# Routed attention and a gelu feed-forward on one Trainium2 core: rounding the weights one operation at a time instead of in blocks

## The chip, the core and the metric

The kernel runs on one core of one Trainium2 chip. A core has a matrix engine (TensorE, in the profile PE, with its weight loads shown as PEld), a vector engine (VectorE, DVE), a scalar engine for activations and copies (ScalarE, ACT), a general engine (GpSimd, POOL) and an engine that issues most transfers (SyncE, SP). They run side by side, each through its own list of instructions in order, and wait for one another through semaphores. On-chip data lies in SBUF; matrix products land in PSUM[...]. The metric is the device time of the whole program in microseconds (us). The kernel before takes 1042.07 us, the median of three runs (1040.81 to 1043.41).

## The reference

What is computed is this:

```python
# q, k, v: (4, 8, 768, 64); centroids: (8, 16, 64)
q_assign = argmax(einsum('bhsd,hcd->bhsc', q_n, c_n))      # nearest centroid
k_assign = argmax(einsum('bhsd,hcd->bhsc', k_n, c_n))
mask = q_assign[:, :, :, None] == k_assign[:, :, None, :]
scores = where(mask, q @ k.T / sqrt(64), -1e9)
attn = softmax(scores) @ v
x = attn.transpose(0, 2, 1, 3).reshape(3072, 512)
h = x @ w_in                                               # 512 x 2048
out = (h / (1 + exp(-1.702 * h))) @ w_out                  # 2048 x 512
```

So there are 4 batches of 8 heads. A query attends only to the keys that share its cluster, and the result goes through a feed-forward block with a quick gelu.

## The kernel before, in words

**Layout.** Heads are handled in pairs; a pair with half of its 768 queries is a group (`g`), and a group has six units (`u`), one for each block of 128 keys. The main loop (L608 to L654) goes through *turns*: each turn `t` takes two units. There are 96 turns, 24 to a batch, 3 to a group. In a turn TensorE does, in this order: the two units' scores (L397), for the first batch the products that bring in the mask (`part`, L411), the products with v of the turn before (`values`, L454), and then pieces of other work: the sums of a group (`normalise`, L466), transposes and centroid products that prepare coming pairs (`prep`, L275 to L345), and pieces of the feed-forward block (`ffn`).

**Beside TensorE.** ScalarE takes exps of the scores (L422). GpSimd adds the exps of a group up (L443, `sum`, 128x768, one addition in a group's first turn and two in its others). From the second batch on VectorE applies the mask (L433). After a group's last unit, TensorE sums over partitions, VectorE takes a reciprocal (L469) and multiplies (L471).

**Feed-forward of the first half batch.** `ffn_half` runs from turn 14, at 1.6 pieces a turn: 16 pieces `first(f)` (L516 to L526) of four matrix products (L520), each followed by a gelu: tanh on ScalarE (L490), then one VectorE operation (L491) that reads the product's PSUM bank; and then 12 pieces `second3` (L528), the products with w_out (L500). The bank pool `ps_m` (tile name `m`) has three banks for all of this: products of the feed-forward, transposes, the group sums. A product can start when an earlier user's last reader has released its bank.

**Rounding of the weights.** The weights come in as 64-bit numbers, in 32 chunks of 128x512 (16 of w_in, then 16 of w_out). `round_next` (L165) rounds one chunk with four VectorE operations: L175 (shift and mask the high half), L178 (put in sign and exponent, two SBUF inputs), L180 (mask out the power of two), L183 (the low half times that power, two SBUF inputs), and one addition (L185) that makes the weight. At its start it asks for the chunk after next (`load_w(i + 2)`, into one of three `raw` buffers), and at its end it puts two checks on ScalarE (`check_w`, L196 and L199). For the last chunk the check writes over the raw data itself. In the eight chunks of turns 0 to 13 the addition is on VectorE. From turn 14 it is on GpSimd, and each turn rounds two chunks: one at the top of the turn, right after the exps (L622), one at the very end (L653), until all 32 are done, in turn 25. Nothing reorders the instructions afterwards (`manual_schedule`): on each engine they stand as the Python code issues them.

The stream of VectorE in turns 14 to 25 is thus: four rounding operations, the mask (from turn 24), the reciprocal (turns 16, 19, 22, 25), an assignment (`prep_assign`, L306 to L329, in turns 21 and 24), one or two gelus, four rounding operations. GpSimd's is: the addition of the top chunk, the exp sums of the turn, the addition of the end chunk.

**After the loop.** The other batches' feed-forward (`first7` and `second7`, L746 and L803) runs when the attention is through.

Of the kernel before, what the change touches and what calls it, by code (L numbers as in the profile page):

```python
# [38 lines left out]
def fast(  # L39
# [26 lines left out]
    nc = tc.nc  # L66
# [40 lines left out]
    def bank():  # L107
        return ps_m.tile([P, 512], FP32, name="m")

    def short():  # L110
        return tmp.tile([P, HALF], FP32, name="short")
# [14 lines left out]
    def load_v(p):  # L126
        b, hp = divmod(p, HP)
        t = pairs.tile([P, 2, NJ, D], FP32, name="inv")
        nc.sync.dma_start(
            out=t.rearrange("p a j d -> p a (j d)"),  # L130
            in_=v[b, 2 * hp:2 * hp + 2].rearrange(
                "a (p j) d -> p a (j d)", j=NJ))
        v_in[p] = t
# [15 lines left out]
    NW = len(w_chunks)  # L149
    w_raw, w_pow = {}, {}  # L150

    def load_w(i):
        if i < NW:
            t = wp.tile([P, WN, 2], I32, name="raw")
            nc.sync.dma_start(out=t.rearrange("p n t -> p (n t)"),
                              in_=w_chunks[i][1])
            w_raw[i] = t
# [4 lines left out]
    POWER = -2 ** 23  # L162
    w_done = [0]

    def round_next(in_psum=False, engine=nc.gpsimd):  # L165

        i = w_done[0]
        if i == NW:
            return
        load_w(i + 2)  # L170
        raw, w = w_raw.pop(i), w_chunks[i][0]
        e = wp.tile([P, WN], I32, name="e", bufs=2)
        a = bank() if in_psum else w
        hi, lo, a_i = raw[:, :, 1], raw.bitcast(U32)[:, :, 0], a.bitcast(I32)
        nc.vector.tensor_scalar(out=a_i, in0=hi, scalar1=3, scalar2=0x3FFFFFF8,  # L175
                                op0=ALU.logical_shift_left,
                                op1=ALU.bitwise_and)
        nc.vector.scalar_tensor_tensor(out=a_i, in0=hi, scalar=ODD, in1=a_i,  # L178
                                       op0=ALU.bitwise_and, op1=ALU.bitwise_or)
        nc.vector.tensor_scalar(out=e, in0=a_i, scalar1=POWER, scalar2=None,  # L180
                                op0=ALU.bitwise_and)
        e = e.bitcast(FP32)
        nc.vector.scalar_tensor_tensor(out=e, in0=lo, scalar=2.0 ** -52, in1=e,  # L183
                                       op0=ALU.mult, op1=ALU.mult)
        engine.tensor_tensor(out=w, in0=a, in1=e, op=ALU.add)  # L185

        check_w(i, raw, w_chunks[NW - 1][0] if i < NW - 1 else raw.bitcast(
            FP32)[:, :, 1])
        w_done[0] += 1

    def check_w(i, raw, z):

        nc.scalar.activation(out=z, in_=raw.bitcast(FP32)[:, :, 1],  # L196
                             func=AF.Square,
                             accum_out=row_sums[:, 2, i:i + 1])
        nc.scalar.activation(out=z, in_=z, func=AF.Exp, scale=-2.0 ** 12,  # L199
                             bias=fifteen[:, 0:1],  # L200
                             accum_out=row_sums[:, 3, i:i + 1])

    def round_to(n):
        while w_done[0] < n:
            round_next()

    load_qk(1, 0)
    load_v(0)
# [252 lines left out]
    def normalise(g):  # L461

        sm = sum_of.pop(g)
        ps = bank()
        for a in range(2):
            nc.tensor.matmul(out=ps[a * D:(a + 1) * D, 0:HALF], lhsT=twos,  # L466
                             rhs=sm[:, a, :], start=True, stop=True)
        rec = recs[g] = short()
        nc.vector.reciprocal(out=rec, in_=ps[:, 0:HALF])  # L469
        x = xT_of[g] = O_of.pop(g)  # L470
        nc.vector.tensor_tensor(out=x, in0=x, in1=rec, op=ALU.mult)  # L471
        if g % HP == HP - 1 and g < 2 * HP:
            (half_ffn, ffn)[g // HP].extend((ffn_half, ffn_tiles)[g // HP]())
# [14 lines left out]
    def gelu(g, t, h):  # L488

        nc.scalar.activation(out=t, in_=h, func=AF.Tanh, scale=1.702)  # L490
        nc.vector.scalar_tensor_tensor(out=g, in0=t, scalar=1.0, in1=h,  # L491
                                       op0=ALU.add, op1=ALU.mult)
# [5 lines left out]
    def second(bh, n, f, g, ps):  # L498

        nc.tensor.matmul(out=ps[:, 0:DM], lhsT=g, rhs=w_out[:, f, :],  # L500
                         start=(f == 0), stop=(f == NF - 1))
        if f == NF - 1:
            b, h = divmod(bh, 2)
            y = yp.tile([P, DM], FP32, name="y")
            nc.scalar.copy(y, ps[:, 0:DM])
            nc.sync.dma_start(out=out_rows(b, h, n), in_=y)

    half_ffn, ffn = deque(), deque()

    def ffn_half():  # L510


        xT = [xT_of.pop(c) for c in range(NCH)]
        gs, ys = {}, {}

        def first(f):  # L516
            round_to((f * P // WN + 1) * NCH)
            ps = bank()
            for c in range(NCH):
                nc.tensor.matmul(out=ps[:, 0:HALF],  # L520
                                 lhsT=w_in[:, c, f * P:(f + 1) * P],
                                 rhs=xT[c], start=(c == 0),
                                 stop=(c == NCH - 1))
            g = gs[f] = (xp.tile([P, HALF], FP32, name="x") if f % 4 else
                         gp.tile([P, 4 * P], FP32, name="g")[:, 0:HALF])
            gelu(g, g, ps[:, 0:HALF])  # L526

        def second3(n, part):  # L528
            round_to(NW // 2 + 4 * (part + 1))
            if part == 0:  # L530
                ys[n] = bank()
            for f in range(4 * part, 4 * part + 4):
                second(0, n, f, (gs.pop(f) if n == NH - 1 else gs[f])[
                    :, n * P:(n + 1) * P], ys[n])

        return ([lambda f=f: first(f) for f in range(NF)]
                + [lambda n=n, q=q: second3(n, q)
                   for n in range(NH) for q in range(NF // 4)])
# [33 lines left out]
    NT = NU // 2  # L572
    TG = NJ // 2
    TB = 2 * HP * TG

    prep_at = {}
    for p in range(1, NPAIR):
        b, hp = divmod(p, HP)
        for i in range(2 if p == 1 else 0, len(PREP)):
            if p == 1:  # L580
                t = (i - 2) // 2
            elif b == 0:
                t = (hp - 2) * TG + 1 + i // 2
            else:
                t = b * TB + TG * hp - (7, 7, 6, 6, 4, 3, 2)[i]
# [5 lines left out]
    def prep(p, i):  # L591
        if i == 0 and p:
            load_v(p)
        PREP[i](p)
        if i in (1, 3) and loads:
            load_qk(*loads.popleft())

    rate = 1.6


    pace = {t: 1 for t in (0, 2, 5, 8, 9, 11, 12, 13)}
    pace.update((t, 2) for t in range(TB // 2 + 2, NT))
    owed = 0.0
    for p, i in [(0, i) for i in range(6)] + [(1, i) for i in range(2)]:
        prep(p, i)
# [2 lines left out]
    for t in range(NT + 2):  # L608
        us = range(2 * t, 2 * t + 2) if t < NT else ()
        for u in us:  # L610
            scores(u)
        if t == 0:
            prep(0, 6)
        for u in us:
            part(u)
        for u in us:
            exps(u)
        second_half = t >= TB // 2
        how = ((False, nc.gpsimd) if t >= TB // 2 + 2 else
               (t > 2, nc.vector))  # L620
        late = t <= 2 or t == TB // 2 + 1
        if pace.get(t) and not late:  # L622
            round_next(*how)
        if recs:
            check(*recs)
        for u in us:
            mask(u)
        work = sorted(prep_at.get(t, ()), key=lambda w: PREP[w[1]] != prep_near)
        while work and PREP[work[0][1]] == prep_near:
            prep(*work.pop(0))  # L630
        if 1 <= t <= NT:
            for u in range(2 * t - 2, 2 * t):
                values(u)

        kept = NF // 2 if t < NT - 3 else NF // 4
        todo = half_ffn or (ffn if len(ffn) > kept else ())
        if not todo:
            owed = 0.0
        elif half_ffn:
            owed += rate  # L640
        else:
            owed += 0.65 if t < NT - 3 else 1.0
        g = (t - 2) // TG if t >= 2 and (t - 2) % TG == TG - 1 else None
        if g is not None and second_half:
            normalise(g)
        for p, i in work:
            prep(p, i)
        if g is not None and not second_half:
            normalise(g)
        while owed >= 1 and todo:  # L650
            todo.popleft()()
            owed -= 1
        if pace.get(t) == 2 or pace.get(t) and late:  # L653
            round_next(*how)  # L654
    check(*recs)
    qcode.clear()
    att.close()
# [648 lines left out]
```

## Time and profile before

| Engine | busy us | share of 1040.6 us |
| --- | --- | --- |
| TensorE (PE) | 993.8 | 96% |
| VectorE (DVE) | 681.7 | 66% |
| GpSimd (POOL) | 418.6 | 40% |
| ScalarE (ACT) | 372.8 | 36% |

| Group | count | mean ns |
| --- | --- | --- |
| L175 on w_out chunks | 16 | 574 |
| L178 on w_out chunks | 16 | 1354 |
| L180 on w_out chunks | 16 | 426 |
| L183, all chunks | 32 | 876 |
| L491 gelu, 128x384 into x | 12 | 550 |
| L469 reciprocal | 32 | 2552 |
| L443 sums (sum<-sum,A) | 128 | 1834 |

Busy times are of the whole span; a TensorE that is busy in the profile is not at its peak all the time, since the ends of its pipelined products are modelled. The turns that concern the change lie between about 86 and 208 us on VectorE; TensorE works on a turn some us before VectorE does. The prediction shows lines of that stretch. In the timelines, columns are: start in us, duration in us, engine, line of the kernel, operation, tile written and tiles read, shapes, how many; in brackets, how long the engine stood idle ahead of it and who ended the wait.

### The profile page before, as it was taken

What the parts mean: (1) busy time and instruction counts of PE and PEld (TensorE: products, weight loads), DVE (VectorE), ACT (ScalarE), POOL (GpSimd) and SP (SyncE); (2) the same over time, 40 slices, a digit from 0 to 9 for tenths busy, and PEclk for the clock granted to TensorE, in tenths of its full rate; (3) what the DMA queues carried; (4) which work ended last, traced back from release to release, by engine and by line L of the source; (5) the groups of instructions that cost most, each with busy time, mean ns of one, the idle gap of its engine ahead of it and who ended that gap; (6) DMA issues with size and microseconds to landing.
All of it is one profiled execution on the core that took longest, in us unless ns stands there. A gap on an engine that the chain in (4) does not pass through costs nothing.

```text
span 1040.6 us, 12560 instructions
## 1 busy us (share of the span) xinstructions
PE 993.8 (96%) x4574; PEld 583.8 (56%) x4574; DVE 681.7 (66%) x1055; ACT 372.8 (36%) x761; POOL 418.6 (40%) x304
## 2 busy tenths in 40 slices
PE   7999888989999999999999999999999999999997
PEld 4434434434554435544454355688755788656886
DVE  4699987844777687677777667744377634576431
ACT  4676564432445544554545222200022100222000
POOL 2574654523566556565666757500022100120000
PEclk9999898999999999999999999999999999999999
DMA  8423544310003310220000000000000000000000
GB/s 222 129 61 101 155 135 136 107 41 18 19 17 76 92 41 2 57 71 27 26 1 1 11 1 0 1 21 21 21 0 1 1 21 21 21 0 1 21 21 23
DMA packets 66118, 45.25 MB, mean 43 GB/s; under 512 B 52096, under 2 KB 60032, under 8 KB 66048
## 3 DMA queue, kind: packets, MB, share of 16 engines
q1 hardware_dynamic: 65904, 44.33, 14.9%
q8 instruction: 38, 0.62, 0.3%
q14 instruction: 32, 0.26, 0.1%
q10 hardware_dynamic: 144, 0.03, 0.0%
HBM read 38.04 MB, written 6.31 MB: 43 GB/s over the span
## 4 chain that ended last, share of the span: by engine, by line
PE 83%; DVE 13%; ACT 2%; issue 1%; DMA 0%; POOL 0%; DVEq 0%; ACTq 0%
PE b L803 21%; PE b L746 21%; PE s L397 11%; PE o L454 10%; PE m L500 7%; PE m L549 4%; PE m L520 3%; PE m L275 2%; DVE short L469 2%; DVE e L183 2%; PE m L466 2%; DVE w_out L178 1%; DVE e L180 1%; DVE A L433 1%; DVE w_in L178 1%
## 5 line engine op out<-in xcount | busy, mean ns | idle before, releaser
L443 POOL TENSOR_TENSOR sum<-sum,A 128x768 f32<-128x768 f32 x128 | 234.7, 1834 | 133.8 <-DVE A L433 115.3
L433 DVE SCALAR_TENSOR_TENSOR A<-qb,code,s 128x384 f32<-128x384 uint8 x288 | 157.4, 608 | 89.4 <-ACT s L422 52.6
L397 PE MATMUL s<-T,T 64*128 64x384 f32 x768 | 154.1, 514 | 2.9 <-DVE A L433 0.6
L454 PE MATMUL o<-A,inv 128*64 128x384 f32 x768 | 145.1, 499 | 1.0 <-ACT x L459 1.0
L422 ACT ACTIVATE s<-s 128x768 f32<-128x768 f32 x144 | 109.0, 793 | 99.5 <-PE s L397 87.1
L737 DVE TENSOR_TENSOR G<-b,G 128x384 f32<-128x384 f32 x168 | 93.4, 556 | 48.3 <-PE b L746 41.4
L684 POOL TENSOR_TENSOR W<-w_in 128x256 f32<-128x256 f32 x24 | 17.7, 738 | 261.0 <-PE b L746 259.3
L490 ACT ACTIVATE th<-G 128x384 f32<-128x384 f32 x96 | 50.2, 523 | 163.4 <-DVE G L737 103.0
L397 PEld LDWEIGHTS s<-T,T 64*128 64x128 f32 x768 | 65.7, 187 | 75.6 <-issue 34.0
L737 DVE TENSOR_TENSOR y<-b,y 128x256 f32<-128x256 f32 x54 | 22.1, 423 | 130.0 <-PE b L803 93.5
L746 PE MATMUL b<-x,w_in 128*128 128x384 f32 x288 | 101.3, 487 | 0.0
L454 PEld LDWEIGHTS o<-A,inv 128*64 128x64 f32 x768 | 46.6, 136 | 85.1 <-issue 81.4
L469 DVE RECIPROCAL short<-m 128x384 f32<-128x384 f32 x32 | 81.7, 2552 | 7.2 <-PE m L466 7.1
L443 POOL TENSOR_TENSOR sum<-A 128x768 f32<-128x768 f32 x32 | 58.8, 1836 | 63.7 <-DVE A L433 32.5
L491 DVE SCALAR_TENSOR_TENSOR G<-th,G 128x384 f32<-128x384 f32 x96 | 68.6, 714 | 16.8 <-ACT th L490 14.2
L746 PEld LDWEIGHTS b<-x,w_in 128*128 128x128 f32 x288 | 54.9, 191 | 37.8 <-issue 0.5
L746 PE MATMUL b<-x,W 128*128 128x384 f32 x192 | 70.7, 492 | 0.0
L803 PE MATMUL b<-Z,G 128*128 128x256 f32 x288 | 65.1, 380 | 0.0
L803 PE MATMUL b<-w_out,G 128*128 128x256 f32 x288 | 63.6, 380 | 0.0
L500 PE MATMUL m<-w_out,g 128*128 128x512 f32 x120 | 60.0, 619 | 2.2 <-ACT T L280 2.2
L520 PE MATMUL m<-x,w_in 128*128 128x384 f32 x128 | 49.3, 542 | 10.3 <-DVE short L309 5.2
L803 PEld LDWEIGHTS b<-w_out,G 128*128 128x128 f32 x288 | 54.7, 190 | 7.9
(126 smaller groups left out, 1343.2 us busy)
## 6 DMA issues: line engine op xcount, KB each, us to landing
raw<-in_moe_w_in_dram SPq DMA_DIRECT2D x16, 512.0 KB, 4.8
raw<-in_moe_w_out_dram SPq DMA_DIRECT2D x16, 512.0 KB, 3.6
in<-in_q_dram SPq DMA_DIRECT2D x32, 192.0 KB, 4.2
in<-in_k_dram SPq DMA_DIRECT2D x32, 192.0 KB, 3.2
inv<-in_v_dram SPq DMA_DIRECT2D x16, 384.0 KB, 4.2
out_dram<-y SPq DMA_DIRECT2D x15, 256.0 KB, 2.5
qb<-line SPq DMA_DIRECT2D x12, 192.0 KB, 3.3
out_dram<-y SPq DMA_DIRECT2D x18, 128.0 KB, 1.8
```

What stands on the lines that cost most here:

```text
L397: nc.tensor.matmul(out=ps[:, a, 0:HALF], lhsT=T[p, 1][rows, kt * P:(kt + 1) * P], rhs=T[p, 0][rows, h * HALF:(h + 1) * HALF], start=True, ...
L422: nc.scalar.activation(out=A_of[u] if p < HP else s, in_=s, func=AF.Exp, scale=SCALE)
L433: nc.vector.scalar_tensor_tensor(out=A_of[u][:, a, :], in0=qcode[p][:, a, h * HALF:(h + 1) * HALF], scalar=code[p][:, kt % NH, 1, kt // NH ...
L443: nc.gpsimd.tensor_tensor(out=sum_of[g], in0=A_of[u - 1] if kt == 1 else sum_of[g], in1=A, op=ALU.add)
L454: nc.tensor.matmul(out=o_of[g][a * D:(a + 1) * D, 0:HALF], lhsT=v_in[p][:, a, kt, :], rhs=A[:, a, :], start=(kt == 0), stop=(kt == NJ - 1))
L469: nc.vector.reciprocal(out=rec, in_=ps[:, 0:HALF])
L491: nc.vector.scalar_tensor_tensor(out=g, in0=t, scalar=1.0, in1=h, op0=ALU.add, op1=ALU.mult)
L500: nc.tensor.matmul(out=ps[:, 0:DM], lhsT=g, rhs=w_out[:, f, :], start=(f == 0), stop=(f == NF - 1))
L520: nc.tensor.matmul(out=ps[:, 0:HALF], lhsT=w_in[:, c, f * P:(f + 1) * P], rhs=xT[c], start=(c == 0), stop=(c == NCH - 1))
L737: nc.vector.tensor_tensor(out=o, in0=p, in1=a, op=ALU.add)
L746: nc.tensor.matmul(out=ps[:, 0:HALF], lhsT=a[:, c], rhs=x(c), start=(c == 0), stop=(c == 1))
L803: nc.tensor.matmul(out=ps[:, 0:DN], lhsT=a(f // 4)[:, f % 4], rhs=z(f), start=(f == 0), stop=(f == FB - 1))
```

## The change

Rounding becomes a generator that hands over one VectorE operation at a time; `step` takes the next one, and the fourth brings the addition and the checks with it. From turn 14 each turn gets a budget of eight steps, as many as two chunks need. `advance(n)` takes up to n of them, and is called at many places of the turn: two steps at the top, one after `normalise`, one after each preparation, three between a feed-forward product and its gelu, two after each feed-forward piece. Before turn 14 a chunk is still rounded in one go. The purpose is to place the rounding where VectorE would wait for TensorE, and to let gelus, reciprocals and preparations not stand behind whole blocks.

```diff
-    def round_next(in_psum=False, engine=nc.gpsimd):
+    def rounding(in_psum, engine):
...
         nc.vector.tensor_scalar(out=a_i, in0=hi, scalar1=3, scalar2=0x3FFFFFF8,
...
+        yield
         nc.vector.scalar_tensor_tensor(out=a_i, in0=hi, scalar=ODD, in1=a_i,
...
+        yield
         nc.vector.tensor_scalar(out=e, in0=a_i, scalar1=POWER, scalar2=None,
...
+        yield
...
         w_done[0] += 1
+        yield
...
+    steps = [0]
+    def advance(n):
+        while n and steps[0] > 0:
+            step()
+            steps[0] -= 1
+            n -= 1
...
+            advance(3)
             gelu(g, g, ps[:, 0:HALF])
...
-    pace.update((t, 2) for t in range(TB // 2 + 2, NT))
...
-        how = ((False, nc.gpsimd) if t >= TB // 2 + 2 else
-               (t > 2, nc.vector))
+        if t > TB // 2 + 1:
+            steps[0] += 8
         late = t <= 2 or t == TB // 2 + 1
         if pace.get(t) and not late:
-            round_next(*how)
+            round_next(True, nc.vector)
+        advance(2)
...
         if g is not None and second_half:
             normalise(g)
+        advance(1)
         for p, i in work:
             prep(p, i)
+            advance(1)
...
         while owed >= 1 and todo:
             todo.popleft()()
             owed -= 1
-        if pace.get(t) == 2 or pace.get(t) and late:
-            round_next(*how)
+            advance(2)
+        if pace.get(t) and late:
+            round_next(t > 2, nc.vector)
```

With it the streams of turns 14 to 25 become, R being one rounding operation, N the reciprocal and its multiplication, A the assignment, M the masks, g a gelu:

```
turn   before            after
14     4R g 4R           6R g 2R
15     4R gg 4R          6R g 2R g
16     4R N g 4R         2R N 4R g 2R
17     4R gg 4R          8R gg
18     4R gg 4R          8R gg
19     4R N g 4R         2R N 4R g 2R
20     4R gg 4R          8R gg
21     4R A g 4R         3R A 5R g
22     4R N gg 4R        2R N 5R g R g
23     4R gg 4R          8R gg
24     4R M A 4R         2R M R A 5R
25     4R M N 4R         2R M N 6R
```

On GpSimd, the exp sums of a turn now stand ahead of both of its weight additions instead of between them.

More of the change, by code (lines that the diff above doesn't have):

```diff
@@ L163, in fast @@
     w_done = [0]
-    def round_next(in_psum=False, engine=nc.gpsimd):
+    def rounding(in_psum, engine):
         i = w_done[0]
-        if i == NW:
-            return
         load_w(i + 2)
@@ L189, in round_next, with step @@
         w_done[0] += 1
+        yield
+    now = []
+    def step(*how):
+        if not now and w_done[0] < NW:
+            now.append(rounding(*(how or (False, nc.gpsimd))))
+        if now:
+            n = w_done[0]
+            next(now[0])
+            if w_done[0] > n:
+                now.clear()
+    def round_next(*how):
+        n = w_done[0]
+        while w_done[0] == n < NW:
+            step(*how)
     def check_w(i, raw, z):
@@ L204, in round_to @@
         while w_done[0] < n:
-            round_next()
+            step()
     load_qk(1, 0)
@@ L508, in fast @@
     half_ffn, ffn = deque(), deque()
+    steps = [0]
+    def advance(n):
+        while n and steps[0] > 0:
+            step()
+            steps[0] -= 1
+            n -= 1
     def ffn_half():
```

## The prediction

> **What bounds the kernel now.** I read the page's slices first, then summed the engines over the turns that the diff touches, then the chain of work, then the VectorE and GpSimd timelines of those turns side by side. From about 215 us on the chain is TensorE almost without a break (TensorE 83% of the span, VectorE 13%), so only what moves the start of that tail moves the end. The slices show where VectorE is fullest and the TensorE clock dips: the third to the eighth of the 40 slices, 52 to 208 us.
>
> ```profile
> PE   7999888989999999999999999999999999999997
> DVE  4699987844777687677777667744377634576431
> PEclk9999898999999999999999999999999999999999
> ```
>
> VectorE issues the first rounding operation of turn 14 at 86.36 us and the last chunk's second one (L178) at 207.90, ended 208.60. Summed over nearly that stretch (columns: window, its length, then busy us and instructions of TensorE, its weight loads, VectorE, ScalarE, GpSimd; clock, DMA share, GB/s):
>
> ```profile
> 86.36:207.45 121.09, 104.06 (x438) 49.44 (x436) 106.92 (x135) 64.92 (x153) 68.01 (x43) 0.93 0.44 132
> ```
>
> VectorE is 88% busy. But the busy time is not all work. The two timelines (start us, us, engine, line) show one block of turn 14:
>
> ```profile
> 88.63 0.55 DVE L491 SCALAR_TENSOR_TENSOR g<-g,m 128x384 f32<-128x384 f32 x1
> 89.09 1.26 DVE L175 TENSOR_SCALAR w_in<-raw 128x512 int32<-128x512 int32 x1
> 90.38 2.19 DVE L178 SCALAR_TENSOR_TENSOR w_in<-raw,w_in 128x512 int32<-128x512 int32 x1
> 92.60 1.92 DVE L180 TENSOR_SCALAR e<-w_in 128x512 int32<-128x512 int32 x1
> 94.56 0.69 DVE L183 SCALAR_TENSOR_TENSOR e<-raw,e 128x512 f32<-128x512 uint32 x1
> 95.17 0.42 DVE L175 TENSOR_SCALAR w_in<-raw 128x512 int32<-128x512 int32 x1
> 95.63 1.65 DVE L178 SCALAR_TENSOR_TENSOR w_in<-raw,w_in 128x512 int32<-128x512 int32 x1
> 97.38 0.43 DVE L180 TENSOR_SCALAR e<-w_in 128x512 int32<-128x512 int32 x1
> ```
>
> ```profile
> 88.79 1.28 POOL L185 TENSOR_TENSOR w_in<-w_in,e 128x512 f32<-128x512 f32 x1 [8.04 <-DVE e L183]
> 90.03 4.21 POOL L443 TENSOR_TENSOR sum<-sum,A 128x768 f32<-128x768 f32 x2
> 95.33 1.40 POOL L185 TENSOR_TENSOR w_in<-w_in,e 128x512 f32<-128x512 f32 x1 [1.09 <-DVE e L183]
> ```
>
> L175 takes 0.42 alone and 1.26 beside GpSimd's add; L178 0.69 and 2.19; L180 0.43 and 1.92: each held operation ends 0.3 to 0.7 us after a GpSimd operation does. The two engines take turns. The gelu L491 reads PSUM and keeps its 0.55. Going through 86.36 to 208.60 operation by operation, time above each operation's shortest is 29.7 us; idle time of VectorE is 9.9 us, in five gaps, each the tanh of a product that TensorE began late, as here (the second line is TensorE's own gap before it):
>
> ```profile
> 163.75 0.56 DVE L491 SCALAR_TENSOR_TENSOR x<-x,m 128x384 f32<-128x384 f32 x1 [3.35 <-ACT x L490]
> ```
>
> ```profile
> 158.36 4.83 PE L520 MATMUL m<-x,w_in 128*128 128x384 f32 x8 [5.16 <-DVE short L309]
> ```
>
> So of 122.2 us, 82.6 are work that no order removes, and 39.6 are held or waiting. The stretch is handed to the tail by ScalarE: the last chunk's check overwrites its own raw data, so it waits for L178 at 208.60, and the exps and copies behind it hold TensorE until 213.35:
>
> ```profile
> 208.63 0.69 ACT L196 ACTIVATE raw<-raw 128x512 f32<-128x512 f32 x1 [10.34 <-DVE w_out L178]
> ```
>
> TensorE itself stands still 21.4 us between 76 and 225 us, so it could run earlier if VectorE did.
>
> **What the Trainium skill says.** "SBUF — State Buffer", section "Who interferes with whom": a VectorE instruction with two SBUF inputs, or a tensor_scalar in a two-port mode, shares an exclusive lock with GpSimd; whoever comes first keeps it for its whole instruction, and an instruction with at most one SBUF input outside those modes isn't held. The trace agrees: 0.43 against 1.92 us for L180, 0.55 always for L491. "Perfetto Trace Analysis", section "GPSIMD Engine Instruction": GpSimd spans are to be timed by the spacing of starts. I therefore take 1.24 us for an add (88.79 to 90.03) and about 1.85 for a sum.
>
> **The change part by part.** The same 96 operations run in turns 14 to 25, eight a turn in both, and TensorE's order and its three `m` banks are the same through turn 23. No instruction is added. Three things move.
>
> (a) Reciprocals (turns 16, 19, 22, 25) and the assignments of turns 21 and 24 stand behind 2 or 3 rounding operations instead of 8. The product of turn 21 waited for the assignment's L309 until 158.22. In the new order, carrying my times below forward, L309 ends near 157.6, TensorE starts there, and five rounding operations fill VectorE until the tanh: the 3.35 us gap shrinks to about 0.35. Of the other gaps (0.64, 1.82, 2.08, 2.03) I keep one of 1.4 in turn 22, before the reciprocal, and fill the rest, since eight operations (or six, in the middle of a split pair) now stand ahead of every first gelu. Idle: 9.9 to 1.75, a gain of 8.1.
>
> (b) First gelus of turns 17 and 20 get ten operations between them and the gelu before (8 before), since two are left over from the reciprocal turn. They come up to 5 us later, and gelus free the banks. But the next turn's bank is wanted only after two products, scores and values, 5.4+3.5 us, so TensorE loses little: 0 to 1 us. I take it as hidden there.
>
> (c) GpSimd's queue now has a turn's exp sums (L443) ahead of both its weight adds, where the first add was ahead of the sums. So after every turn's eighth operation GpSimd runs add, sum, sum back to back, just when VectorE starts the next turn's rounding, with nothing but 0 to 2 gelus (0.47 each) between. Before, the sums met the gelus, the reciprocal or an idle gap. Prices, all from this trace: an add in the middle of a stream holds 0.95 (1.64 less 0.69); add, sum, sum against a stream hold 0.85+1.49+1.50 = 3.84 (the fence); a second sum beside a 2.55 us reciprocal holds nothing; a gelu ahead takes 0.1 to 0.3 off the add, two take 0.6. One sum instead of two in turns 15, 18, 21, 24.
> - Turns 17, 20: 3.84+0.95 = 4.8 each; turn 23, behind a gelu, 4.5; turn 14, whose sums now run before it, 0.95. Sum 15.05.
> - Turn 15: 0.85+1.5+0.95 = 3.3; turns 18, 21: 0.3+1.5+0.95 = 2.75 each; turn 24, whose sum waits for masks, 1.7. Sum 10.5.
> - Turns 16, 19, 22, 25, with a reciprocal: 3.2, 2.7, 2.0, 2.9. Sum 10.8.
> - L312 and L329 as now: 1.6; turn 14's sums against turn 13's L471: 0.5.
>
> Held: 38.5, against 29.7, a loss of 8.8. With (a): 38.5+1.75 = 40.2 against 39.6. Following the same operations turn by turn on paper, with each held operation's end at the GpSimd operation's end, puts the last L178 at 207.6 instead of 208.6. The two ways differ by 1.6 us, which is what such working can resolve; I take the middle, half a us earlier: 1041.5. The bounds on (c): 30 (as held as now) and 47 (every turn at full price without gelus: 0.95+3*4.8, 4*3.3, 4*3.2, and 5 for the rest). On (a): 0 and 5 us left idle.
>
> Chunk loads: issued when the chunk three earlier is done, landed some 3.6 us later (85.79 to 89.42). In both orders two whole chunks lie between, at least 4.6 us of work (0.42+0.69+0.43+0.69 each, with the starts' spacing), and a turn's gelus. Nothing. The checks on ScalarE (1.6 us a chunk) move in front of a tanh that waits for its product anyway; ScalarE is 54% busy. Nothing.
>
> **The rivals.**
> 1. Gaps go (9.9 to 1) and holds stay near 30 because sums find reciprocals and gelus. 39.6 to 31 is 8.6 earlier, near 1033.5. For: TensorE's 21 us of standing still are ready to be filled. Against: rounding is what holds worst, and it now sits beside the sums.
> 2. Holds become the bound: 47 plus 3 idle against 39.6, 10 later, with TensorE starved and its clock cold at each stall (81.35: 2.85 for eight matmuls, 158.36: 4.83) perhaps 1 more: near 1051. A milder form, half of that, gives 1046. For: every rounding operation can be held. Against: the sums run somewhere in both orders.
>
> **How the numbers follow.** Forecast 0.45, rival 1 0.30, rival 2 0.25. The forecast case spreads by some 3 us, so three quarters of it lie within 0.3% (3.1 us), with an eighth on each side; with the mild edges of the rivals: faster 0.35, same 0.38, slower 0.27. The range 1031 to 1049 leaves out the far half of rival 2 and the best of rival 1.
>
> **What would show it.** L178, L175 and L180 of turns 14 to 25 held by 35 to 40 us in all (right), under 31 or over 45 (rivals). VectorE's gaps there under 3 us. GpSimd add, sum, sum back to back after a turn's last rounding operation. The chunk-31 check on ScalarE still waiting for VectorE, at 207 to 209 us. TensorE's tail unchanged in length. I'd be wrong if sums were delayed past the rounding, if TensorE had to wait on the later gelus of turns 17 and 20, or if the tail, whose bank order differs from turn 24 on, changed.

## The result, and the profile after

The changed kernel takes 1038.24 us (median of four runs, 1037.74 to 1039.07); the kernel before took 1041.78 in the same comparison. The ratio is 0.9965, with a 95% interval of 0.9948 to 0.9982: 3.5 us faster, where 1041.5 had been forecast. It lies inside the stated range, a little outside the 0.3% within which the prediction put three quarters of its own case.

The slices of the page after the change, the same three rows as before:

```profile
PE   7998879899999999999999999999999999999997
DVE  4699998943677687677777667734377534576431
PEclk9999998999999999999999999999999999999999
```

VectorE's full stretch is fuller (in slices 4 to 7, 9998 where it was 9987), and the clock dips in one slice instead of two. The sum over turns 14 to 25, from the first rounding operation of turn 14 to the end of the last chunk's L178 (columns as before; lines of the changed kernel are up to 32 higher, R1 to R4 are its L174, L178, L181, L185):

```profile
86.59:205.78 119.19, 103.22 (x420) 48.71 (x416) 112.65 (x137) 67.50 (x157) 66.82 (x41) 0.93 0.43 134
```

119.2 us instead of 122.2. Adding up the same 136 VectorE operations of both kernels, each split into its shortest duration, what it is longer than that (held), and the time between it and the one before:

| us | before | after |
| --- | --- | --- |
| shortest durations | 82.3 | 81.9 |
| held | 29.7 | 35.9 |
| idle, gaps over 0.15 | 9.9 | 3.2 |
| small gaps less overlaps | +0.3 | -1.8 |
| sum | 122.2 | 119.2 |

The first two rows depend on what counts as shortest: with one set of shortest durations for both kernels they are 82.0 and 82.0, then 30.0 and 35.8. Either way the exchange that the prediction described took place: idle time went and held time came. Turn 17 in the VectorE timeline after the change, from its first operation on:

```profile
112.14 0.42 DVE L174 TENSOR_SCALAR w_in<-raw 128x512 int32<-128x512 int32 x1
112.60 1.65 DVE L178 SCALAR_TENSOR_TENSOR w_in<-raw,w_in 128x512 int32<-128x512 int32 x1
114.35 1.84 DVE L181 TENSOR_SCALAR e<-w_in 128x512 int32<-128x512 int32 x1
116.22 2.18 DVE L185 SCALAR_TENSOR_TENSOR e<-raw,e 128x512 f32<-128x512 uint32 x1
118.33 0.41 DVE L174 TENSOR_SCALAR w_in<-raw 128x512 int32<-128x512 int32 x1
118.78 1.65 DVE L178 SCALAR_TENSOR_TENSOR w_in<-raw,w_in 128x512 int32<-128x512 int32 x1
```

and GpSimd at the same time:

```profile
112.30 1.39 POOL L187 TENSOR_TENSOR w_in<-w_in,e 128x512 f32<-128x512 f32 x1 [2.15 <-DVE e L185]
113.65 4.20 POOL L463 TENSOR_TENSOR sum<-sum,A 128x768 f32<-128x768 f32 x2
118.48 1.39 POOL L187 TENSOR_TENSOR w_in<-w_in,e 128x512 f32<-128x512 f32 x1 [0.63 <-DVE e L185]
```

Add, sum, sum stand back to back behind a turn's last rounding operation, and hold R2, R3 and R4 by 0.95, 1.43 and 1.50 us, then the middle add holds R2 again by 0.95: 4.83, where the prediction had 4.8. The two gaps that are left on VectorE:

```profile
162.69 0.56 DVE L511 SCALAR_TENSOR_TENSOR x<-x,m 128x384 f32<-128x384 f32 x1 [1.12 <-ACT x L510]
166.40 2.56 DVE L489 RECIPROCAL short<-m 128x384 f32<-128x384 f32 x1 [2.09 <-PE m L486]
```

How VectorE's 3.0 us reach the end is seen on TensorE. I take the start of each turn's first scores product on TensorE, counted from that of turn 14:

| us on TensorE | before | after |
| --- | --- | --- |
| turns 14 to 23 together | 106.7 | 104.2 |
| turn 24 | 9.5 | 13.0 |
| turn 25 | 10.8 | 10.8 |
| turn 26 | 14.0 | 8.4 |
| turns 14 to 26 together | 141.0 | 136.4 |

TensorE gains 2.5 us, loses 3.5 in turn 24, and comes to turn 26 a us *later* than before. All that reaches the tail is won in turn 26 alone, 5.6 us. From turn 27 to the end the kernels take the same, 821.6 us before and 821.5 after. TensorE in turns 24 and 26, first before (two stops, and the first eight-matmul piece of turn 26 begins with 1.92 for two):

```profile
190.53 1.13 PE L500 MATMUL m<-w_out,g 128*128 128x512 f32 x2 [1.71 <-ACT T L280]
...
213.35 0.70 PE L275 MATMUL m<-ident,in 128*128 128x128 f32 x3 [4.14 <-ACT short L295]
213.85 1.92 PE L500 MATMUL m<-w_out,g 128*128 128x512 f32 x2
```

and after:

```profile
190.06 2.05 PE L520 MATMUL m<-w_out,g 128*128 128x512 f32 x2 [3.68 <-DVE short L329]
...
210.55 0.55 PE L295 MATMUL m<-ident,in 128*128 128x128 f32 x3 [0.24 <-ACT short L315]
210.93 1.02 PE L520 MATMUL m<-w_out,g 128*128 128x512 f32 x2
```

The stop of turn 26 is nearly gone (0.24 us), and with it the slow clock behind it: 1.02 us for two matmuls instead of 1.92. From the stop to turn 27 the granted clock was 0.70 before and 1.00 after. The stop of turn 24 doubled, with a new releaser: VectorE's L329 (an operation of the assignment) instead of a copy on ScalarE. Going by that releaser, the pool chose another bank for the first product with w_out. And ScalarE's last check, which hands VectorE's stretch over, starts earlier:

```profile
205.81 0.68 ACT L216 ACTIVATE raw<-raw 128x512 f32<-128x512 f32 x1 [4.96 <-DVE w_out L178]
```

So the path of before is still there: the check starts when VectorE's last L178 ends, and TensorE goes on 4.7 us after that, at 213.35 before (check at 208.63) and at 210.55 after. VectorE's last L178 ends 2.8 us earlier, and TensorE goes on 2.8 us earlier. From there to turn 27 it needed 5.6 us before and 3.9 after, another 1.7. The short stop has a second side: TensorE also came a us later, so that its own arrival at this place and the end of the wait now lie only 0.24 us apart.

### The profile page after: what moved, and what is told of

Its sections match the earlier page's. It is cut to its first block, busy times and chain, and to the rows that moved or that the text cites. A ratio compares the mean times of both kernels' runs of the same rounds, so it can differ in the third digit from the quotient of the medians.

```text
span 1035.9 us, 12558 instructions
## 1 busy us (share of the span) xinstructions
PE 994.2 (96%) x4574; PEld 583.1 (56%) x4574; DVE 686.6 (66%) x1055; ACT 374.0 (36%) x761; POOL 421.3 (41%) x304
## 4 chain that ended last, share of the span: by engine, by line
PE 80%; DVE 16%; ACT 1%; issue 1%; DMA 0%; SPq 0%; DVEq 0%; ACTq 0%
PE b L835 21%; PE b L778 21%; PE s L417 11%; PE o L474 10%; PE m L520 7%; PE m L577 4%; DVE e L185 3%; DVE w_out L178 2%; DVE short L489 2%; PE m L295 2%; DVE e L181 2%; PE m L486 2%; DVE w_in L178 1%; DVE A L453 1%; PE m L309 1%
## 5 line engine op out<-in xcount | busy, mean ns | idle before, releaser
L835 PEld LDWEIGHTS b<-Z,G 128*128 128x128 f32 x288 | 54.8, 190 | 7.4
```

Source lines behind the costliest of these rows:

```text
L835: nc.tensor.matmul(out=ps[:, 0:DN], lhsT=a(f // 4)[:, f % 4], rhs=z(f), start=(f == 0), stop=(f == FB - 1))
```

## The experiments

At first I held theory 1: VectorE's stretch decides, and the change shortens it by trading idle for held time. Its rivals here, which are not those of the prediction: the early reciprocals alone (rival 1), GpSimd's order (rival 2), and the one handover in turn 26 (rival 3). In all runs the whole output is computed. Ratios are to the kernel before on the same chip.

**Early blocks alone.** Edit of the kernel before:

```diff
-        if pace.get(t) and not late:
+        if pace.get(t) == 1 and not late:
             round_next(*how)
...
             normalise(g)
+        if pace.get(t) == 2:
+            round_next(*how)
         while owed >= 1 and todo:
```

> The kernel before, with its blocks of four kept whole; from turn 14 the block at the top of a turn stands behind the turn's reciprocal and preparation. So reciprocals and assignments wait behind 4 rounding operations instead of 8, and GpSimd has a turn's sums ahead of both weight additions, as in the changed kernel, but no operation stands alone between product and gelu. Theory 1 (the change exchanges VectorE's idle time for time held by GpSimd, and the rest comes from single operations that fit between dependent ones): held time 34 to 38 us in turns 14 to 25, idle 4 to 7, total 1039 to 1042. Rival (the early reciprocals and assignments are the whole gain): total 1037.5 to 1038.5, idle under 4, held as in the changed kernel.

Measured: 1037.0 us, ratio 0.9943 (0.9927 to 0.9960); held 31.9, idle 1.4, VectorE's stretch 115.5 us. No operation stands alone between product and gelu, and VectorE is 3.6 us *quicker* than in the changed kernel. Rival 1 has this one: the early reciprocals and assignments, with blocks whole, shorten the stretch more than single operations do. The held time was foreseen by neither side (rival 1 had the change's 35.9, theory 1 34 to 38). Yet the total is no better than that of the change by more than the intervals, and TensorE shows why. ScalarE's line, and TensorE's:

```profile
202.30 0.66 ACT L196 ACTIVATE raw<-raw 128x512 f32<-128x512 f32 x1 [13.19 <-DVE w_out L178]
```

```profile
207.01 0.90 PE L275 MATMUL m<-ident,in 128*128 128x128 f32 x3 [8.45 <-ACT short L295]
```

TensorE came to turn 26 at 194.3 us, 11 earlier than before, and stood 8.45 us in it, behind a ScalarE that waited 13.19 us with its check of the last chunk. It went on 4.7 us after that check began, as before: here the end of VectorE's stretch still sets the end of the program.

**Sums between the additions.** In the changed kernel the exp sums of a turn are kept and issued behind the turn's first weight addition:

```diff
-        nc.gpsimd.tensor_tensor(out=sum_of[g],
-                                in0=A_of[u - 1] if kt == 1 else sum_of[g],
-                                in1=A, op=ALU.add)
+        held.append((sum_of[g], A_of[u - 1] if kt == 1 else sum_of[g], A))
+        if not steps[0] or w_done[0] == NW:
+            add_held()
...
             if w_done[0] > n:
                 now.clear()
+                add_held()
```

> The changed kernel, with VectorE's order as it is; in turns 14 to 25 GpSimd's exp sums stand behind the first weight addition of their turn, between the two additions, as they did before the change. Theory 1 (any order that lays a stream of rounding beside GpSimd's sums is held about as much): held time 34 to 40 us, since the sums leave the reciprocals of turns 16, 19, 22 and 25 and meet rounding there; total 1037 to 1041. Rival 2 (the place of the sums ahead of both additions is what raised the held time from 29.7 to 35.9 us): held time 28 to 31, total 1032 to 1035.

Measured: 1045.26 us, ratio 1.0025 (1.0018 to 1.0032); held 44.3, idle 2.5. Rival 2 falls: the order before the change isn't better once VectorE's order is the new one, it is 8 us of held time worse, more even than theory 1 had. The VectorE timeline shows a reciprocal turn, where the sums now miss the reciprocal; the addition holds R2, and the sums behind it hold R3 and R4, round the gelu:

```profile
110.44 1.66 DVE L178 SCALAR_TENSOR_TENSOR w_in<-raw,w_in 128x512 int32<-128x512 int32 x1
112.02 0.54 DVE L519 SCALAR_TENSOR_TENSOR x<-x,m 128x384 f32<-128x384 f32 x1
112.49 1.58 DVE L181 TENSOR_SCALAR e<-w_in 128x512 int32<-128x512 int32 x1
114.10 2.19 DVE L185 SCALAR_TENSOR_TENSOR e<-raw,e 128x512 f32<-128x512 uint32 x1
```

**Additions on VectorE.** In the changed kernel, one word:

```diff
-            now.append(rounding(*(how or (False, nc.gpsimd))))
+            now.append(rounding(*(how or (False, nc.vector))))
```

> The changed kernel with the 24 weight additions of turns 14 to 25 on VectorE instead of GpSimd. Theory 1 (the lock): some 22 holds of 0.95 us by these additions go, 21 us; 24 additions of 0.69 us (0.61 from start to start) come, 14.6 us, and some are held by sums, up to 3 us: VectorE is done 3 us earlier, total 1034 to 1038. Rival (VectorE is bound by its own work and the holds would show elsewhere): 10 to 15 us slower, 1048 to 1053.

Measured: 1035.4 us, ratio 0.9929 (0.9909 to 0.9950), runs from 1031.5 to 1040.0; held 15.9, down by 20.0 (21 expected). 23 additions in the stretch bring 15.9 us of work, and VectorE is 4.7 us quicker (114.5). In turn 17, R2 behind a chunk's addition takes 0.69 us instead of 1.65:

```profile
116.98 0.69 DVE L178 SCALAR_TENSOR_TENSOR w_in<-raw,w_in 128x512 int32<-128x512 int32 x1
```

That is the lock, by an experiment, in this order: the work moved onto the fuller engine, and the engine got done sooner. (The profile is of the quickest execution, 1031.5 us.)

**A free check of the last chunk.** In the kernel before:

```diff
-        check_w(i, raw, w_chunks[NW - 1][0] if i < NW - 1 else raw.bitcast(
-            FP32)[:, :, 1])
+        check_w(i, raw, w_chunks[NW - 1][0] if i < NW - 1 else yp.tile(
+            [P, DM], FP32, name="y"))
```

> The kernel before, but the check of the last weight chunk writes its squares and exps into the output tile y, which is free then, instead of over its own raw data: ScalarE no longer waits for VectorE's L178 of chunk 31. Rival 3 (most of the gain of the change is this one handover: TensorE's stop of 4.1 us in turn 26 and the slow clock behind it): TensorE's stop falls to 1 or 2 us, the eight matmuls after it take 3.8 us instead of 5.4, total 1036.5 to 1038.5. Theory 1 (the backlog of VectorE in turns 14 to 25 is what counts, and would be handed over by the masks of turn 26 instead): 1040 to 1042.

Measured: 1035.04 us, ratio 0.9923 (0.9908 to 0.9938), more than the whole change brings, though VectorE's stretch is as long as before (122.2 us, held 29.7, idle 9.8). TensorE in turn 26:

```profile
211.04 1.22 PE L275 MATMUL m<-ident,in 128*128 128x128 f32 x6
212.09 1.02 PE L500 MATMUL m<-w_out,g 128*128 128x512 f32 x2
```

No stop, full clock. Theory 1's claim that VectorE's backlog is handed on in any case falls: VectorE is as late as before, and with the check free TensorE goes through turn 26 without waiting for it. What is left of theory 1 is that VectorE decides as long as the check waits for it.

**The change on top of a free check.** The same edit in the changed kernel.

> The changed kernel with the last chunk's check writing into y, so that ScalarE doesn't wait for VectorE in turn 26. Handover theory (the change gains only because its VectorE is done in time for that one check; in turns 14 to 25 TensorE gains nothing): TensorE's stop in turn 26 was already 0.24 us, so nothing changes, 1037 to 1039, and the change on top of a free check is 2 to 4 us slower than the kernel before with a free check (1035.0). Rival (theory 1, gains add up): 1030 to 1033.

Measured: 1037.54 us, ratio 0.9946 (0.9934 to 0.9958), against 0.9923 for the kernel before with that edit. The gains don't add up. As the handover theory had it, the change is worth nothing beyond its effect on that check. By the medians it is some 2 us worse on top of a free check, though the two intervals just overlap. It keeps the 3.68 us stop of turn 24.

**Early blocks and a free check.** The edits of the first and the fourth run together.

> Blocks of four kept whole, the top block behind reciprocal and preparation, and the last chunk's check in y. In the run with early blocks alone TensorE reached turn 26 at 194.3 us but stood 8.45 us in it behind ScalarE's check, and worked at the slow clock after. Handover theory: that stop falls under 2 us, turn 27 begins near 204 instead of 212.7, total 1027 to 1031. Rival (VectorE's backlog is handed over by the masks of turn 26 instead): the stop moves to the products with v of turn 27, total 1034 to 1037.

Measured: 1029.99 us, ratio 0.9877 (0.9862 to 0.9892), the quickest of all, 8 us below the changed kernel. Turns 14 to 23 take 96.9 us on TensorE (106.7 before, 104.2 after), and turn 26 takes 11.7 instead of the 18.4 of the early blocks alone; its first stop is now short, and a second one is new:

```profile
200.09 0.55 PE L275 MATMUL m<-ident,in 128*128 128x128 f32 x3 [1.19 <-ACT short L295]
...
205.27 1.12 PE L500 MATMUL m<-w_out,x 128*128 128x512 f32 x2 [2.02 <-POOL w_out L185]
```

The second stop is VectorE's backlog by another way: GpSimd's addition of the last chunk ends just before. And these two gains nearly add up: 0.57% for the early blocks, 0.77% for the free check, 1.23% for both.

**The same with additions on VectorE.** `engine=nc.vector` in both places where turns 14 on choose it.

> The kernel of early blocks and free check, with the 24 weight additions of turns 14 to 25 on VectorE as well. Lock theory: held time falls from some 32 to 15 us, additions cost 14.6 us, so VectorE is done 1 to 4 us earlier; TensorE, which stands still less there, gains 0 to 3 us: 1026 to 1030. Rival (VectorE's work counts): 1035 or more.

A miss: 1036.2 us, ratio 0.9936 (0.9924 to 0.9948). The held time fell from 31.9 to 19.9 only, less than the additions cost (15.9), and idle rose from 1.4 to 6.6. Part of it is seen: blocks of five are held by sums at other places, and late gelus stop TensorE for up to 5.9 us:

```profile
112.39 4.21 PE L520 MATMUL m<-x,w_in 128*128 128x384 f32 x6 [5.90 <-DVE x L491]
```

Why the same move pays with single operations and not with blocks isn't settled.

**All eight at the top.** In the changed kernel `advance(2)` at the top of a turn becomes `advance(8)`.

> The changed kernel with all eight rounding operations of a turn together at its top, ahead of masks, reciprocal, preparation and gelus: between gelus VectorE's order is that of the kernel before, but GpSimd has the sums ahead of both additions. Theory 1 on its part (c): GpSimd's add, sum, sum after the eighth operation meet gelus and reciprocals in part, as now in the kernel before, and the rest meets the next eight; held 33 to 40 us, idle 7 to 10 as before, VectorE done 3 to 8 us later than before, total 1043 to 1050. Rival (GpSimd's order costs nothing, the place of single operations is the gain): as the kernel before, 1041 to 1044, held 28 to 31.

Measured: 1043.37 us, ratio 1.0009 (0.9995 to 1.0022). It answers another question than it was made for. Held time is 28.4 us in a stretch that ends before turn 25's masks and reciprocal, idle 17.4, well over the 7 to 10 expected. The profile is of an execution of 1047.6 us, 4 above the median. Part of the wait is ScalarE's: both chunks' checks, 3.2 us, now stand ahead of the copies that preparation needs, and in turn 23 TensorE waits. In other turns it waits for VectorE, for up to 4.78 us. Turn 23:

```profile
186.15 8.13 PE L547 MATMUL m<-x,w_in 128*128 128x384 f32 x16 [3.23 <-ACT short L315]
```

So where `step` drops the checks in ScalarE's order can matter. How much of the loss that is was not tried, and GpSimd's order isn't separated here.

**The bank of turn 24.** The changed kernel with a free check, in which turns 24 and 25 round in blocks again. Going by what released it, the first product with w_out then gets the bank that it had before.

```diff
-        if t > TB // 2 + 1:
+        if TB // 2 + 1 < t < TB:
             steps[0] += 8
...
+        if t >= TB:
+            round_next()
         advance(2)
...
             round_next(t > 2, nc.vector)
+        if t >= TB:
+            round_next()
```

> The changed kernel with a free check of the last chunk, in which turns 24 and 25 round in blocks as before the change, so that the first product with w_out in turn 24 gets the bank that it had before (released by a ScalarE copy) instead of that of the assignment (released by L329 on VectorE). Bank theory (the changed kernel's 3.68 us stop in turn 24 and the slow clock behind it are a price of the bank that the pool chose): turn 24 takes 9.5 us on TensorE instead of 13.0 to 14.4, total 1033.5 to 1035, 3 us below the changed kernel with a free check. Rival (the stop only hides VectorE's backlog, which shows in the next turns instead): 1036.5 to 1038.

Measured: 1032.41 us, a us below what I expected, ratio 0.9889 (0.9871 to 0.9908). Turn 24 takes 8.4 us (14.4 with the free check alone), and TensorE's stop there 0.65. Bank and order of two turns were changed together, so the bank alone wasn't tried; but turns 14 to 23 are those of the changed kernel, and what it loses in turn 24 is got back.

**The same without the free check.**

> The same without the free check. Handover theory: TensorE comes to turn 26 about 3 us earlier than in the changed kernel and gives most of that back there, since ScalarE's last check still waits for VectorE's L178 of chunk 31 at 205 us or so: total 1036.5 to 1038.5, no better than the changed kernel by more than 1.5 us. Rival (a gain of TensorE up to turn 25 reaches the end): 1034 to 1035.

Measured: 1039.19 us, ratio 0.9959 (0.9943 to 0.9974); the time is over the figure I gave, on a chip where the kernel before took 1043.65. Turn 24 takes 8.4 us again, and turn 26 takes 13.7: what TensorE won is lost in the stop behind the check. The two runs differ by the free check alone: 6.8 us, of which turn 26 has 5.7.

```profile
188.62 1.13 PE L520 MATMUL m<-w_out,g 128*128 128x512 f32 x2 [0.66 <-ACT T L300]
...
211.15 0.79 PE L295 MATMUL m<-ident,in 128*128 128x128 f32 x3 [3.84 <-ACT short L315]
```

## Why the prediction was right, and where it was wrong

- *Part (a), idle time.* 9.9 to 1.75 forecast, 3.2 measured. The assignment's L309, L329 in the changed kernel, was done at 156.5 (157.6 forecast), the gap behind it 1.12 (0.35), the gap ahead of turn 22's reciprocal 2.09 (1.4). Mechanism right, size 1.5 us too hopeful.
- *Part (b), later gelus in turns 17 and 20.* They came up to 4 us later (g at 121.60 against 117.58), and TensorE began turn 18's products at 122.67 against 122.20. In turn 21 it stood 1.44 us behind a gelu of turn 20, but then waited 4.06 more for the assignment, as it had before (5.16). Hidden, as forecast.
- *Part (c), the GpSimd order.* 38.5 held forecast, 35.9 measured. The prices hold turn by turn: 0.95 in turn 14, 3.3 in turn 15, 4.83 in turns 17 and 20, 2.8 in turn 18. Too dear were turn 22, where the sums found VectorE's gap (0.95 for 2.0), turn 25, and the assignments' small operations. That part of the sum was mis-sized by 2.6.
- *A term that was missing.* Single operations beside independent neighbours took 2.1 us less between them. Together, VectorE's stretch came 3.0 us shorter; the sum had said 0.6 longer, the walk on paper 1.0 earlier.
- *Sums.* The upper bound of (c), called 47, adds up to 46.4. And the middle of 0.6 us later and 1.0 earlier is 0.2 earlier, not the half a us that was forecast. With the two ways pointing opposite ways, that the direction came out right owes something to luck.
- *The step that failed* is the tail: "TensorE's tail unchanged in length", and the gain at the end taken as equal to that of the last L178. The end got 4.6 us in the profiles, of which 2.8 are that L178. Nearly all of the rest is the clock: with the stop of turn 26 down from 4.14 to 0.24 us, TensorE needed 3.9 us instead of 5.6 from there to turn 27. The tail from turn 27 on did keep its length. The wait that I had named, the check on ScalarE, was the right one. What I had not asked is how long TensorE would stand there, and whether VectorE's backlog mattered without it. With a free check it cost the kernel before nothing in turn 26, and the early blocks 2.02 us by way of the last addition.
- *The checks: "Nothing".* True in the changed kernel, where no stop of TensorE in turns 14 to 25 ends on ScalarE; not in general, as eight operations at the top showed.
- *"If the tail, whose bank order differs from turn 24 on, changed"* was listed as a way to be wrong. It did: 3.5 us on TensorE in turn 24, hidden in the result because turn 26 waited for VectorE anyway, as the last two runs showed.
- *Rivals of the prediction.* Its rival 1 had idle gone and held near 30, which the early blocks reached (1.4 and 31.9), not this change; its rival 2 had 47 held, which the sums between the additions came near to (44.3).

## What to carry to other kernels

When one engine runs behind in a stretch and another catches up after it, look for the single wait that hands the delay over, and try to take that wait away besides reordering the stretch: writing the last check elsewhere brought 0.8%, this reordering 0.35% and nothing on top of it, the better reordering 0.57% alone and both together 1.23%. At such a wait the later of two engines decides, and a gain on one counts only as far as the other lets it. A queue order changes more than the engine that it was meant for: here also the lock that VectorE shares with GpSimd, ScalarE's order, and the bank that a pool hands out. Count time from stage to stage on the engine that bounds the end, since an engine can be quicker over a stretch and the end not know of it.

## What the runs showed of the hardware

- Two VectorE operations of which the second needs the first's output start 0.03 to 0.11 us after its end; independent ones start up to 0.09 before it. In the VectorE timeline after the change, a gelu behind R2 (ends at 90.95, gelu at 90.86), where R3 behind R2 waits for 0.10 (92.84+1.65 = 94.49, then 94.59):

```profile
89.30 1.65 DVE L178 SCALAR_TENSOR_TENSOR w_in<-raw,w_in 128x512 int32<-128x512 int32 x1
90.86 0.54 DVE L511 SCALAR_TENSOR_TENSOR g<-g,m 128x384 f32<-128x384 f32 x1
```

- "TensorE: Matmul & The Clock Gate" of the Trainium skill, section "What's actually happening", has the clock fall to half after an idle window of some 3.4 us. Here TensorE was slow after stops of 4.14 and 3.68 us, but in the changed kernel also after 2.71 and 2.86: eight matmuls that take 2.85 took 4.15 at a granted clock of 0.67, and sixteen took 7.12 instead of 5.43 at 0.76. So a stop of under 3 us can already cost 1.3 to 1.7 us. It need not: after a stop of 2.13 before the change eight matmuls took 2.85, and after one of 2.80 in the last experiment sixteen took 5.43 at a clock of 1.00.
- Moving 24 additions from GpSimd to VectorE made VectorE quicker by 4.7 us in one order and slower by 8.9 in another (124.5 against 115.6).
